# Score matmuls in tiles of 64 by 32 from the third group of heads on, and one pair of vector sums moved behind two copies, in a fused attention and feed-forward kernel

## The chip, the cores and the metric

The kernel runs on one NeuronCore of a Trainium2 chip. The metric is the device time of one execution in microseconds (us). Before the change three runs took 413.71, 417.81 and 420.57 us (median 417.81). The profile is of one further execution, which took 417.34 us.

## The reference, cut to what matters

Attention with normed queries and keys, then a feed-forward layer. Batch 8, 12 heads, 448 positions, head size 64:

```python
q_n, k_n = (rmsnorm(q, g_q), rmsnorm(k, g_k))
scores = scale * np.matmul(q_n, k_n.transpose(0, 1, 3, 2))
scores = scores - np.max(scores, axis=-1, keepdims=True)
attn = np.exp(scores)
attn = attn / (np.sum(attn, axis=-1, keepdims=True) + 1e-09)
x = np.matmul(attn, v)          # to (3584, 768), heads side by side
h = x @ w_in                    # (768, 2048)
g = np.maximum(h, 0.0) + alpha * np.minimum(h, 0.0)
out = g @ w_out                 # (2048, 768)
```

## The kernel before

**Groups.** The unit of attention work is a group `y` of four heads (two heads `par` in each of two halves `g`), 24 groups in all, three to a batch. One call of `score(y, j)` (line 355) makes the scores of the four heads for 64 keys against all 448 queries, into one PSUM tile `sc` of two banks (two such buffers). `soft` (line 373) exponentiates that tile on ScalarE, in one instruction of about 1 us. A group has seven such tiles.

**How a score tile is cut.** In `score`, the stationary operand has 64 rows (the head size) and `m` columns (keys). For groups 0 to 8 (`EARLY` is 9) `m` is 64: four matmuls of form 64*64, one for each head. From group 9 on `m` is 32: eight matmuls of form 64*32. Each moves the same 448 queries, and each is two instructions on TensorE's queue, a weight load and a matmul.

**Sums over the keys.** The denominators (`den`, `den_pre`, lines 419 and 424) and the products with v (`attv`, line 446) are 56 matmuls each, through `over_keys` or `ones_over` (lines 381 and 402), all of them of form 64*32 in every group. `den` puts its sums in the bank pair with tag "acc". `den_pre` is for the third group of a batch, which is handled alone: it puts them in the two single banks with tag "mm" and copies both at once to SBUF on VectorE (line 430), so that those banks come free. Then ScalarE takes logarithm and exponential of the copies (`log_pre`, `invert`), and VectorE multiplies them with the products (line 486, `muls`).

**The feed-forward work.** `up` (matmuls on line 501, form 128*128, tiles `hT`) is followed by a ScalarE and a VectorE instruction; `down` (line 563, `op`) by a VectorE copy and two output DMAs. From batch 2 on, the second product is done in three parts, `quad_a`, `quad_b`, `quad_c` (lines 641 to 692, matmuls on line 628), with seven block products in place of eight. They need sums and differences of blocks of g for each pair of output tiles: `mix_two` (lines 603 to 617) makes `s1` and `s2`, on VectorE in the calls spoken of here, and `mix_rest` (lines 619 to 624) makes two more on GpSimd. `quad_a` uses `s2` in its third product, `quad_b` uses `s1` and one of the GpSimd results. Products and `den_pre` take turns in the same two "mm" banks: a product can't begin before the bank was read out by VectorE.

**The order.** The program is written out by hand for every engine. A planner makes a list of 69 bursts; each has two to four score tiles and at most one step of denominators (`dens`) and one of products with v (`avs`). Between bursts lie feed-forward units (`gaps`), from burst 28 on by a written table (lines 942 to 948). `prep` holds calls that come at a burst's start, ahead of its score tiles, and `jobs` holds VectorE work that is put between other steps. The `mix_two` and `mix_rest` of seven pairs of output tiles are put in `prep` of the bursts 33, 36, 41, 48, 55, 57 and 62 by the loop on line 971. Of these seven bursts only 36 has a `den_pre` (group 11). Its order on VectorE before the change: `mix_two(8)` (two instructions), the two copies of the denominators, two reductions (`jobs`), then what `quad_a(8)` needs.

What calls what around the change, at the start of a burst `n`:

```python
for f, a in prep.get(n, ()):
    f(*a)
...
sums = n in dens and pre(dens[n])
if sums:
    den_pre(dens[n])
    for f, a in jobs.pop(n, ()):
        f(*a)
    ...
    attv(avs[n], 0, False, (log_pre, invert), put, ...)
```

**Loads.** Queries and keys of later groups, v, `w_in` and `w_out` are loaded while the first bursts run: `load_qk` on the queue of SP, `load_v`, `load_w_in` and `load_w_out` on that of GpSimd.

Of the kernel before, what the change touches and what calls it, by code (L numbers as in the profile page):

```python
# [21 lines left out]
def kernel(  # L22
# [12 lines left out]
    nc = tc.nc  # L35
# [15 lines left out]
    EARLY = 3 * G  # L51
# [300 lines left out]
    def pre(ys):  # L352
        return len(ys) == 1 and ys[0] >= PRE and ys[0] % G == G - 1

    def score(y, j):
        qT, kT = qkT[y, "q"], qkT[y, "k"]
        sc = pss.tile([128, 2, 512], FP32, name="sc", tag="sc")
        m = 64 if y < EARLY else 32
        for c in range(64 // m):
            for par in range(2):  # L360
                for g in range(2):
                    nc.tensor.matmul(  # L362
                        out=sc[ds(64 * g + m * c, m), par, :S].rearrange(
                            "p (j c) -> p j c", j=J
                        ),
                        lhsT=kT[ds(64 * par, 64), j, g, ts(c, m)],
                        rhs=qT[ds(64 * par, 64), :, g, :],
                        start=True,
                        stop=True,
                    )  # L370
        scs[y, j] = sc
# [27 lines left out]
    def cols_of(ys):  # L399
        return S // 2 if halved(ys) else S  # L400

    def ones_over(accs, ys):

        if not halved(ys):
            return over_keys(accs, ys, lambda g, y, par, c, j: ones[ds(64 * g, 64)])
        for j in range(J):
            for c in range(2):
                for par in range(2):
                    for g in range(2):
                        p = ds(64 * g, 64)  # L410
                        nc.tensor.matmul(
                            out=accs[g][ds(64 * c + 32 * par, 32), : S // 2],
                            lhsT=ones[p],
                            rhs=expT[ys[0]][p, j, par, ts(c, S // 2)],
                            start=(j == 0),
                            stop=(j == J - 1),
                        )

    def den(ys):
        dn = psa.tile([128, 2, 512], FP32, name="dn", tag="acc")  # L420
        ones_over((dn[:, 0], dn[:, 1]), ys)
        rden[ys] = dn

    def den_pre(ys):
        accs = [psf.tile([128, 512], FP32, name="dnb", tag="mm") for _ in range(2)]
        ones_over(accs, ys)
        r = att.tile([128, 2, S], FP32, name="rden", tag="rden")[:, :, : cols_of(ys)]
        rden[ys] = r
        for g in range(2):
            nc.vector.tensor_copy(out=r[:, g], in_=accs[g][:, : cols_of(ys)])  # L430
# [15 lines left out]
    def attv(ys, half, spare=False, jobs=(), put=None, early=False):  # L446

        b, i = divmod(ys[0], G)
        v2 = vt[b].rearrange("p h j (d e) -> p h j d e", e=2)

        def weights(g, y, par, c, j):
            h = 2 * (y - G * b) + par
            return v2[ds(64 * g, 64), h, j, :, half if len(ys) == 2 else c]

        if half:
            av, accs = None, [psf.tile([128, 512], FP32, name="avb", tag="mm") for _ in range(2)]
        else:
            pool, tag = (pss, "sc") if spare else (psa, "acc")
            av = pool.tile([128, 2, 512], FP32, name="av", tag=tag)
            accs = (av[:, 0], av[:, 1])  # L460
        over_keys(accs, ys, weights)
        for f in jobs:
            f(ys)
        if b not in xT:
            xT[b] = att.tile([128, 2, G, S], FP16, name="xT", tag="xT")
        x, r = xT[b][:, :, i + half, :], rden[ys]
        if half:
            for g in range(2):
                nc.vector.tensor_mul(out=x[:, g], in0=accs[g][:, :S], in1=r[:, g])
        else:  # L470
            parts = [(x, av[:, :, :S], r)]
            if halved(ys):
                parts = [
                    (x[ds(64 * e, 64), :, c], av[ds(64 * e, 64), :, c], r[ds(64 * n, 64)])
                    for n, c in enumerate(ts(n, S // 2) for n in range(2)) for e in range(2)
                ]
            if put is not None:
                soon = 2 if early else 0
                muls(parts[:soon])
                put.append((muls, (parts[soon:],)))  # L480
            else:
                muls(parts)
# [292 lines left out]
    bursts, dens, avs, first_in, last_in = [], {}, {}, {}, {}  # L775
# [5 lines left out]
    m = 0  # L781
    while m < NG * J or steps:
        n = len(bursts)
# [20 lines left out]
        while len(bursts[n]) < limit and m < NG * J:  # L804
            y, j = divmod(m, J)
# [13 lines left out]
    def at(n, f, *a):  # L819
        prep.setdefault(max(int(n), 0), []).append((f, a))  # L820
# [14 lines left out]
    for y in range(G, NG):  # L835

        early = y < G + 2
        if early:
            n = turn_at[y - 1] + 1
        elif y == G + 2:  # L840
            n = den_at[G - 1]
        elif y == 2 * G:
            n = turn_at[y] - 4
        elif y % G == 1:
            n = den_at[y - 4] - 1 - pre((y - 2,))
        elif y % G:
            n = den_at[y - G] - pre((y - G,))
        else:
            n = av_at[y - 4]
# [98 lines left out]
    ).split("|")  # L948
    quads = {"a": quad_a, "b": quad_b, "c": quad_c}

    forced = set()

    def units(line):
        for w in line.split():
# [14 lines left out]
    rest = list(units("b20 c20 u16"))  # L969
    assert not downs and not ups  # L970
    for n, y in ((33, 6), (36, 8), (41, 10), (48, 12), (55, 14), (57, 16), (62, 18)):
        at(n, mix_two, y, nc.vector)
        at(n, mix_rest, y)
    at(65, mix_two, 20, nc.vector, "nat")
# [75 lines left out]
    for n in range(NB):  # L1050
# [6 lines left out]
        for t in first_tiles:  # L1057
            if t == (0, J - 2):
                spin(1)
            elif t == (1, J - 3):  # L1060
                spin(2, False)
            elif t == (1, J - 2):
                spin(1, False)
            elif t == (0, J - 1):
                turn_one(1, "q")
            elif t == (1, 0):
                turn_one(1, "k")
            elif t == (1, J - 1):
                turn(2)
            score(*t)  # L1070
            if n == den_at[G - 1] - 1 and t == tiles[-1]:
                begin(0)
                begin(1)
            elif lead and t == tiles[0]:
                soft(*t)
                den(dens[n])
                attv(avs[n], 0, True, (log, invert))
            elif lead and t == tiles[1]:
                begin(2)
# [11 lines left out]
        sums = n in dens and pre(dens[n])  # L1091
        if sums:
            den_pre(dens[n])
            for f, a in jobs.pop(n, ()):
                f(*a)
            put = [] if not gaps[n] or gaps[n][0][0] in (quad_a, quad_c) else None
            attv(avs[n], 0, False, (log_pre, invert), put, gaps[n] and gaps[n][0][0] is quad_c)
            if not gaps[n]:
                last_jobs, put = [(muls, (p,)) for _, (ps,) in put for p in (ps[:2], ps[2:])], None
            elif put and gaps[n][0][0] is quad_a:  # L1100
                put.insert(0, (lambda: None, ()))
            if put:
                jobs[n] = put + jobs.get(n, [])
        elif n in dens and not lead:
            den(dens[n])
# [4 lines left out]
        for t in () if lead else tiles[len(first_tiles) : 3]:  # L1110
            score(*t)
            soft(*t)
        if n in avs and len(avs[n]) == 2 and avs[n] != (0, 1):
            attv(avs[n], 1)
        for t in () if lead else tiles[max(len(first_tiles), 3) :]:
            score(*t)
            soft(*t)
# [3 lines left out]
        if n in roots:  # L1121
            y = roots[n]
# [112 lines left out]
```

## Time and profile before

| what | us |
|---|---|
| runs before | 413.71, 417.81, 420.57 |
| the profiled execution, its own time | 417.34 |
| its span, first to last instruction | 415.6 |
| outside the span | 1.74 |
| TensorE busy, matmuls | 398.9 (96%), 5055 instructions |
| TensorE weight loads | 208.3 (50%), 5055 instructions |
| VectorE, ScalarE, GpSimd busy | 265.8, 273.4, 255.2 |
| mean granted TensorE clock | 0.994 of full speed |

In the lines of the profile, PE is TensorE, PEld its weight loads, DVE VectorE, ACT ScalarE, POOL GpSimd and SP the engine whose queue issues most DMAs. A line of the timeline gives the start, the time from the first start to the last end, the instructions' engine, line of the kernel, operation, out<-in, form and number, and in brackets how long the engine had been idle before, and what ended that. "issue" stands for a wait that nothing in the profile ended. Ends of matmuls are modelled and overlap the next ones, so the distance from start to start is what a step costs.

### The profile page before, as it was taken

What the parts mean: (1) busy time and instruction counts of PE and PEld (TensorE: products, weight loads), DVE (VectorE), ACT (ScalarE), POOL (GpSimd) and SP (SyncE); (2) the same over time, 40 slices, a digit from 0 to 9 for tenths busy, and PEclk for the clock granted to TensorE, in tenths of its full rate; (3) what the DMA queues carried; (4) which work ended last, traced back from release to release, by engine and by line L of the source; (5) the groups of instructions that cost most, each with busy time, mean ns of one, the idle gap of its engine ahead of it and who ended that gap; (6) DMA issues with size and microseconds to landing.
All of it is one profiled execution on the core that took longest, in us unless ns stands there. A gap on an engine that the chain in (4) does not pass through costs nothing. (4 is left out here: it accounts for less than half of the span.)

```text
span 415.6 us, 11768 instructions
## 1 busy us (share of the span) xinstructions
PE 398.9 (96%) x5055; PEld 208.3 (50%) x5055; DVE 265.8 (64%) x421; ACT 273.4 (66%) x390; POOL 255.2 (61%) x180
## 2 busy tenths in 40 slices
PE   6889899999999999989999999999999999999996
PEld 3344345544455445544455445444555445655564
DVE  3876675575556485795788585958577755465322
ACT  4798697778956785666786897884667884135110
POOL 5589695779596974887094857476633507400870
PEclk9899999999999999999999999999999999999999
DMA  8999999976827596829957596279412800320133
GB/s 182 238 234 229 162 210 168 231 193 88 178 36 177 136 125 112 182 64 175 141 81 175 130 211 139 67 167 193 95 41 48 141 4 21 77 58 0 38 95 96
DMA packets 68019, 53.39 MB, mean 128 GB/s; under 512 B 35568, under 2 KB 67456, under 8 KB 67968
## 3 DMA queue, kind: packets, MB, share of 16 engines
q1 hardware_dynamic: 53520, 39.54, 45.5%
q0 software_dynamic: 13472, 11.81, 20.0%
q10 hardware_dynamic: 976, 1.31, 1.3%
q8 instruction: 39, 0.64, 0.7%
q14 instruction: 12, 0.10, 0.1%
HBM read 45.62 MB, written 11.01 MB: 136 GB/s over the span
## 5 line engine op out<-in xcount | busy, mean ns | idle before, releaser
L376 ACT ACTIVATE expT<-sc,expb 128x896 f16<-128x896 f32 x168 | 162.2, 1003 | 45.9 <-PE sc L362 45.7
L501 PE MATMUL hT<-xT,w_in_sb 128*128 128x448 f16 x546 | 113.7, 353 | 2.1 <-issue 1.7
L501 PEld LDWEIGHTS <-w_in_sb 128*128 128x128 f16 x768 | 72.7, 98 | 76.6 <-issue 12.3
L545 DVE TENSOR_TENSOR gT<-hT,gT 128x448 f16<-128x448 f32 x91 | 56.6, 623 | 40.3 <-ACT gT L541 39.2
L210 POOL TENSOR_TENSOR qs<-nat,rr 128x896 f16<-128x896 f32 x36 | 60.5, 1702 | 34.7 <-issue 21.8
L182 POOL TENSOR_TENSOR sq<-nat 128x896 f32<-128x896 f32 x32 | 53.5, 1683 | 41.8 <-DMA nat<-in_q_dram 29.6
L541 ACT ACTIVATE gT<-hT,cols 128x448 f16<-128x448 f32 x90 | 56.9, 633 | 30.0 <-PE hT L501 29.7
L362 PE MATMUL sc<-qT,kT 64*32 64x448 f16 (+1 forms) x1092 | 53.7, 358 | 4.3 <-ACT expT L376 2.0
L628 PEld LDWEIGHTS <-gT 128*128 128x128 f16 x352 | 33.5, 98 | 26.8 <-issue 5.7
L501 PE MATMUL hTa<-xT,w_in_sb 128*128 128x448 f16 x210 | 45.4, 353 | 0.0
L190 DVE TENSOR_REDUCE ss<-sq 128x14 f32<-128x896 f32 (+1 forms) x37 | 38.5, 1052 | 0.9 <-POOL sq L182 0.8
L486 DVE TENSOR_TENSOR xT<-av,rden 64x448 f16<-64x448 f32 (+1 forms) x37 | 27.2, 734 | 14.2 <-PE av L387 8.9
L545 DVE TENSOR_TENSOR gT<-hTa,gT 128x448 f16<-128x448 f32 x35 | 21.8, 623 | 19.5 <-ACT gT L541 19.2
L541 ACT ACTIVATE gT<-hTa,cols 128x448 f16<-128x448 f32 x35 | 22.2, 635 | 18.2 <-PE hTa L501 18.1
L362 PEld LDWEIGHTS <-kT 64*32 64x32 f16 (+1 forms) x1092 | 16.0, 93 | 36.0 <-issue 29.9
L563 PE MATMUL op<-w_out_sb,gT 128*128 128x384 f16 x160 | 27.4, 326 | 0.0
L387 PEld LDWEIGHTS <-vt 64*32 64x32 f16 x1344 | 19.9, 92 | 12.4 <-issue 2.8
L616 POOL TENSOR_TENSOR gs<-gT 128x1024 f16<-128x1024 f16 x3 | 6.4, 2125 | 30.4 <-DVE gT L545 28.1
L563 PEld LDWEIGHTS <-gT 128*128 128x128 f16 x192 | 18.0, 98 | 13.4 <-issue 2.3
L387 PE MATMUL av<-expT,vt 64*32 64x448 f16 x896 | 24.3, 350 | 0.3 <-DVE osb L676 0.3
L624 POOL TENSOR_TENSOR gT<-gT 128x1024 f16<-128x1024 f16 x11 | 23.4, 2128 | 0.0
L628 PE MATMUL qx<-w_out_sb,gT 128*128 128x384 f16 x120 | 20.8, 326 | 1.2 <-DVE rden L430 1.2
(149 smaller groups left out, 494.0 us busy)
## 6 DMA issues: line engine op xcount, KB each, us to landing
out_dram<-osb SPq DMA_DIRECT2D x107, 96.0 KB, 3.0
nat<-in_q_dram SPq DMA_DIRECT2D x40, 224.0 KB, 4.2
nat<-in_k_dram SPq DMA_DIRECT2D x40, 224.0 KB, 5.1
vt<-in_v_dram POOLq DMA_DIRECT2D x16, 336.0 KB, 8.0
w_in_sb<-in_moe_w_in_dram POOLq DMA_DIRECT2D x12, 256.0 KB, 7.8
w_out_sb<-in_moe_w_out_dram POOLq DMA_DIRECT2D x4, 768.0 KB, 9.7
arena<-in_q_dram SPq DMA_DIRECT2D x6, 224.0 KB, 7.4
arena<-in_k_dram SPq DMA_DIRECT2D x6, 224.0 KB, 6.8
```

The source lines that it names most:

```text
L182: nc.gpsimd.tensor_mul(out=sqf[:, c], in0=src[:, c], in1=src[:, c])
L190: nc.vector.tensor_reduce(out=o[:, c], in_=sqs[y, nm][:, c], axis=AXIS_X, op=ALU.add)
L210: eng.tensor_mul(out=t.rearrange("p j h d -> p h j d"), in0=nat[y, nm], in1=rr_t[y][:, "qk".index(nm)].unsqueeze(3).broadcast_to((128, 2, ...
L362: nc.tensor.matmul(out=sc[ds(64 * g + m * c, m), par, :S].rearrange("p (j c) -> p j c", j=J), lhsT=kT[ds(64 * par, 64), j, g, ts(c, m)], r ...
L376: nc.scalar.activation(out=expT[y][:, j], in_=scs[y, j][:, :, :S], func=AF.Exp, scale=QK_SCALE, bias=expb[:, 0:1],)
L387: nc.tensor.matmul(out=accs[g][ds(32 * n, 32), :S], lhsT=weights(g, y, par, c, j), rhs=expT[y][ds(64 * g, 64), j, par, :], start=(j == 0), ...
L486: nc.vector.tensor_mul(out=x, in0=av, in1=r)
L501: nc.tensor.matmul(out=hT[:, :S], lhsT=w_in_sb[:, g * G + i, ts(ft, 128)], rhs=xT[b][:, g, i, :], start=(i == 0 and g == 0), stop=(i == G ...
L541: nc.scalar.activation(out=g, in_=hT[:, :S], func=AF.Copy, scale=alpha_sb[:, ft : ft + 1])
L545: nc.vector.tensor_max(out=g, in0=hT[:, :S], in1=g)
L563: nc.tensor.matmul(out=op[:, :OH], lhsT=gT[:, ft, ts(tile % J, 128)], rhs=w_out_sb[:, ft, ts(oh, OH)], start=(ft == 0), stop=(ft == NF - 1),)
L628: nc.tensor.matmul(out=bank[:, c], lhsT=g[:, ft], rhs=v[:, ft, c], start=(first and ft == 0), stop=(ft == HF - 1), skip_group_check=True,)
```

## The change

Two edits. `score` uses 64*64 tiles for groups 0 and 1 alone; groups 2 to 8 (49 score tiles) are cut as the later groups were. And in a burst that has a `den_pre`, the pair `mix_two`, `mix_rest` is no longer called at the burst's start but right behind `den_pre`, that is behind the two copies on VectorE and ahead of the burst's `jobs`. This is the case in burst 36 alone.

```diff
     def score(y, j):
         qT, kT = qkT[y, "q"], qkT[y, "k"]
         sc = pss.tile([128, 2, 512], FP32, name="sc", tag="sc")
-        m = 64 if y < EARLY else 32
+        m = 64 if y < 2 else 32
         for c in range(64 // m):
...
-    forced = set()
+    forced, behind = set(), {}
...
     for n, y in ((33, 6), (36, 8), (41, 10), (48, 12), (55, 14), (57, 16), (62, 18)):
+        if n in dens and pre(dens[n]):
+            behind[n] = [(mix_two, (y, nc.vector)), (mix_rest, (y,))]
+            continue
         at(n, mix_two, y, nc.vector)
         at(n, mix_rest, y)
...
         sums = n in dens and pre(dens[n])
         if sums:
             den_pre(dens[n])
+            for f, a in behind.pop(n, ()):
+                f(*a)
             for f, a in jobs.pop(n, ()):
                 f(*a)
```

## The prediction

> **What bounds the kernel now.** I read the page's busy times, then TensorE's timeline from end to end, then VectorE's and GpSimd's around burst 36, then counts of instructions by window and the DMA queues.
>
> ```profile
> PE 398.9 (96%) x5055; PEld 208.3 (50%) x5055; DVE 265.8 (64%) x421; ACT 273.4 (66%) x390; POOL 255.2 (61%) x180
> DMA  8999999976827596829957596279412800320133
> q8 instruction: 39, 0.64, 0.7%
> ```
>
> TensorE is busy 96% and no other engine over 66%: what shortens TensorE's stream shortens the kernel, and each of its waits lengthens it. DMA is full for the first 83 us (eight slices of 10.4 us). The queue that brings instructions had 39 packets (16 KB each).
>
> TensorE's timeline, once with 64*64 scores around denominators and once with 64*32 scores:
>
> ```profile
> 68.67 0.57 PE L362 MATMUL sc<-qT,kT 64*64 64x448 f16 x8
> 69.17 1.52 PE L387 MATMUL dn<-expT,ones 64*32 64x448 f16 x56
> 70.62 0.38 PE L362 MATMUL sc<-qT,kT 64*64 64x448 f16 x4
> 70.93 2.77 PE L563 MATMUL op<-w_out_sb,gT 128*128 128x384 f16 x16
> ```
>
> ```profile
> 157.21 0.57 PE L362 MATMUL sc<-qT,kT 64*32 64x448 f16 x16
> 157.60 1.51 PE L387 MATMUL dn<-expT,ones 64*32 64x448 f16 x56
> 158.92 0.37 PE L362 MATMUL sc<-qT,kT 64*32 64x448 f16 x8
> 159.23 2.77 PE L563 MATMUL op<-w_out_sb,gT 128*128 128x384 f16 x16
> ```
>
> Start to start the same work takes 70.93 - 68.67 = 2.26 us above and 159.23 - 157.21 = 2.02 below: each border between the two forms costs 0.12 us. Between 128*128 work both forms cost the same: two tiles take 0.50 us start to start either way.
>
> Burst 36, TensorE and VectorE:
>
> ```profile
> 177.72 0.57 PE L362 MATMUL sc<-qT,kT 64*32 64x448 f16 x16
> 179.50 2.76 PE L628 MATMUL qx<-w_out_sb,gT 128*128 128x384 f16 x16 [1.21 <-DVE rden L430]
> 185.93 1.46 PE L628 MATMUL qz<-w_out_sb,gT 128*128 128x384 f16 x8 [0.32 <-DVE osb L657]
> ```
>
> ```profile
> 176.26 2.09 DVE L616 TENSOR_TENSOR arena<-gT 128x1024 f16<-128x1024 f16 x1
> 178.45 0.69 DVE L617 TENSOR_TENSOR arena<-arena,gT 128x1024 f16<-128x1024 f16 x1
> 179.06 0.68 DVE L430 COPY rden<-dnb 128x224 f32<-128x224 f32 x2
> 179.66 2.07 DVE L190 TENSOR_REDUCE ss<-sq 128x14 f32<-128x896 f32 x2
> ```
>
> The product waits for the copies, which stand behind `mix_two`. The longest wait after the start-up is another:
>
> ```profile
> 36.28 0.63 PE L362 MATMUL sc<-qT,kT 64*64 64x448 f16 x4
> 43.33 0.92 PE L501 MATMUL hT<-xT,w_in_sb 128*128 128x448 f16 x4 [1.72 <-issue]
> ```
>
> ```profile
> 36.40:43.20 6.80, 5.21 (x128) 2.56 (x128) 1.59 (x2) 3.77 (x4) 6.67 (x8) 1.00 1.14 218
> ```
>
> At 43.33 TensorE waits though its data is there (xT, line 486, ended at 41.45). At 36.28 a score tile takes 0.63 where others take 0.38: its second weight load comes 0.25 us late. Between the two stoppings lie 128 matmuls and 128 weight loads, 256 instructions exactly; counted from the start they are numbers 705 and 961 of TensorE's queue. An instruction packet began 33.76 and took 1.17 us (TensorE went on 1.59 after its end); the next began 40.87 and took 0.94 (went on 1.52 after). So TensorE's instructions come in blocks of 256; a block is asked for when the one before it is begun, and under full DMA comes about 6.8 us later. Numbers 705 + 256k are the borders; the other packets fit this to the end.
>
> **The change part by part.**
>
> *Borders removed.* From 68 us on, where TensorE otherwise doesn't wait: two around the denominators at 69.17; four around the two sums 74.14 and 75.90 (4.03 us, the same block at 165.83 takes 3.53); two each at 81.09, 85.41 and 111.22; three at 118.79 and 120.55. Fifteen by 0.124 = 1.86 us. Two of these places also hold waits of 0.15 and 0.18 for VectorE, which would grow by what is saved; I take 1.7 (ends 1.5 and 1.86). The borders before 43 us I cost at nothing: the waits for ScalarE's exponentials and for instructions cover them.
>
> *Instructions added.* 49 tiles by 4 matmuls and 4 weight loads are 392. In time they cost nothing between 128*128 work (0.50 against 0.50), and no DMA of the data is added. But every block of 256 now reaches less far in the program.
>
> Block at 705: five tiles of group 2 come before it (40 instructions), so it now begins at what was number 665, a transpose at 33.43. It is asked for at the same place as before, within 0.3 us (29.5 for 29.7), behind the same loads, so TensorE goes on at about 36.2. Then: three transposes, two score tiles, eight `hT` matmuls, group 3's tile; the denominators need two exponentials of 1.0 us behind those score tiles, and start at 38.8 (36.84 before); they and two thirds of the sums with v (1.32 + 0.9) lead to number 961, now what was 897, at 41.0. The next block was asked for at 36.2 and, by the earlier 6.8 us, is there at 43.1. What then still lies before the `hT` of 43.33: 19 matmuls of sums (0.45), a score tile (0.31), eight `hTb` matmuls (1.51). It starts at 45.4: +2.1 us. Ends: 0, if the block comes 2.8 us sooner; 3.0, if it comes as much later as packets differ (0.9).
>
> Block at 1729: 26 tiles come before it, so it begins at what was 1521, at 73.67, just before the sums of 74.14, where instructions go fastest; it ends at what was 1761, at 77.35, after 3.7 us. A block is asked for some 23 instructions ahead of its border (an estimate, from packets that began before TensorE reached theirs). The packets of the two borders nearest (70.62 and 76.70) began at 74.48 and 80.72, 4.35 and 4.24 after that point. Asked for at 73.1, with 4.2 + 0.97 + 1.55 it is there at 79.8: TensorE waits +2.4 us. Ends 0 and 3.0.
>
> The other borders keep a slack of 0.5 us or more by the packets nearest in time, but for one: block 165.84 to 169.07. There DMA is idle from 163 to 167 us, and a packet under idle DMA (120.90, asked for at 120.55) came 0.35 later; with 1.2 and 1.55 that is 168.9, just in time. I take 0; ends 0 and 0.9.
>
> *Burst 36.* `mix_two` and, on GpSimd, `mix_rest` move past the two copies and nothing else; no DMA moves, GpSimd's order stays (its squares until 177.80 come first). The sums of the denominators end at 176.4, so the copies (0.38 each, as in the five other bursts) run at 176.6 to 177.3. `mix_two`'s first took 2.09 here, 0.69 in other bursts; it ended 0.55 after GpSimd's square ended (177.80). It still ends near 178.35, the second at 179.1. So `mix_rest` is no later. The first product starts at 178.2, not 179.50: 1.28 sooner. But VectorE is solid: reductions 179.1 to 181.1, then the copy of the first product at 181.05 (181.64 before), which frees the bank of the third (181.65 for 182.24), and so on to the wait at 185.93. What is late next is VectorE's own row, and the gain left is the copies' 0.6 us. Ends: 0 and 1.6 (both waits gone).
>
> *Sum.* 417.34 (span 415.6 and 1.74 around it) + 2.1 + 2.4 - 1.7 - 0.6 = 419.5 us. The profiled execution is 0.5 below the median of the runs shown, 417.81.
>
> **The rivals.**
>
> *Instructions come in time.* Blocks are asked for sooner in the new order and both waits stay away or merge into the one at 43.33: 417.34 - 1.86 - 0.6 = 414.9. For it: only two of 39 borders stop TensorE now. Against: both are stopped with no slack left (0.25 and 1.87 us), and the new blocks are 2.8 and 3 us shorter in time. It decides once a block comes within 3.7 us of its asking. [...]
>
> *One of the two stays away.* 419.5 - 2.1 or - 2.4: about 417.2. The first is better founded (it stands on a stop that exists), the second on two packets near by.
>
> *Slower: a clock stage on top.* From 7.90 to 11.31 us TensorE was busy 1.07 of 3.41 us, and from 11.31 to 14.73 the granted clock was 0.50. If the wait at 77.35 leaves a stretch of 3.41 us as empty, the next 3.41 run at half: +1.7, 421.2. Against: the wait is 2.4 us, so at least 1.0 us of the stretch is busy and it must fall so; the least busy stretch afterwards, 2.12 (42.03 to 45.45), kept 1.00. The first wait can trip it too, but the second block's arrival covers that.
>
> **How the numbers follow.** Both waits 0.50 (419.5; its own range 417.5 to 421.5), one of them 0.22 (417.2), none 0.17 (414.9), with a clock stage 0.11 (421.2). With the ends of the terms these reach from 414 to 423; 414.5 to 422.5 leaves out less than 2 in 10. A measurement of this kernel can tell about 2% from no change, 8.4 us: none of the cases goes so far, so faster 0.01, same 0.97, slower 0.02.
>
> **What would show it.** Scores of group 2 on as 64*32, PE x5251; the denominators of 69.17 with 1.32 for 1.45 from start to start. An "issue" wait of 2 to 3 us on transposes near 33.5, one in sums (`av`) near 41, one on a score tile or `opa` near 79. In burst 36 the two copies right behind the denominators and ahead of L616, and `qx` without its 1.21. Wrong: if there is no wait by "issue" between 75 and 85 us, the second term goes; if `hT` still starts near 43.3, the first.

## The result, and the profile after

The changed kernel takes 420.16 us (median of 20 runs, 416.63 to 421.05), the kernel before, run beside it, 416.78 us (20 runs, 413.06 to 420.57). The ratio is 1.0087, interval 1.0065 to 1.0110: slower by 0.9%, 3.4 us between the medians, and inside the 2%. The forecast of 419.5 us lay 0.7 below the median. Here and below, medians are over all runs, while ratios leave disturbed runs out and are not quotients of these medians, so that the two can differ by up to 0.3%.

The profiled execution of the changed kernel took 416.63 us (span 414.9). It is the shortest of the 20, so what the change did can't be read from its end. Stages are compared below over several profiles, from landmarks that leave the start-up out (the first denominators start at 26.06 us here and at 27.54 in the profile before).

The page after, first line of part 1, and the instruction queue:

```profile
PE 396.5 (96%) x5251; PEld 209.1 (50%) x5251; DVE 264.4 (64%) x421; ACT 272.8 (66%) x390; POOL 255.4 (62%) x180
q8 instruction: 41, 0.67, 0.7%
```

5251 matmuls are 196 more, 49 tiles by four, and two more packets of instructions come. TensorE's busy time falls by 2.4 us and the others' hardly move, so what is lost must be waits.

TensorE's timeline, changed kernel, around the first two borders:

```profile
31.51 0.79 PE L335 MATMUL tps<-ident,arena 128*128 128x128 f16 x11
34.40 0.34 PE L335 MATMUL tps<-ident,arena 128*128 128x128 f16 x3 [2.10 <-issue]
...
38.32 1.12 PE L387 MATMUL av<-expT,vt 64*32 64x448 f16 x37
40.59 0.74 PE L387 MATMUL av<-expT,vt 64*32 64x448 f16 x19 [1.15 <-issue]
...
42.98 0.92 PE L501 MATMUL hT<-xT,w_in_sb 128*128 128x448 f16 x4
```

Counted from the start, the first instruction after each "issue" wait is number 705 and number 961 of TensorE's queue. They fall on the transposes and in the sums with v that the prediction named, and the `hT` that stood behind the old wait of 1.72 now starts with none. Two waits of 2.10 and 1.15 us are there in place of 0.25 and 1.72. This `hT` starts at 42.98, close to its 43.33 before; but counted from the first denominators it is 16.92 us, 15.79 before.

The same view, at the denominators and at the third border:

```profile
68.32 0.57 PE L362 MATMUL sc<-qT,kT 64*32 64x448 f16 x16
68.71 1.51 PE L387 MATMUL dn<-expT,ones 64*32 64x448 f16 x56
70.03 0.37 PE L362 MATMUL sc<-qT,kT 64*32 64x448 f16 x8
70.34 2.77 PE L563 MATMUL op<-w_out_sb,gT 128*128 128x384 f16 x16
...
76.29 0.35 PE L362 MATMUL sc<-qT,kT 64*32 64x448 f16 x1
77.17 0.38 PE L362 MATMUL sc<-qT,kT 64*32 64x448 f16 x7 [0.53 <-issue]
```

Scores, denominators and scores now take 70.34 - 68.32 = 2.02 us (2.26 before): two borders between forms less, 0.12 each. The stop in the score tile is number 1985 (705 + 5 x 256). There the block ends that the prediction calls the one at 1729, and the expectations below name the stop by that number.

Burst 36, TensorE, first the denominators in the kernel before, then the changed kernel:

```profile
175.66 0.85 PE L411 MATMUL dnb<-expT,ones 64*32 64x224 f16 x56
```

```profile
175.85 0.85 PE L411 MATMUL dnb<-expT,ones 64*32 64x224 f16 x56
...
178.41 2.77 PE L628 MATMUL qx<-w_out_sb,gT 128*128 128x384 f16 x16
181.86 1.46 PE L628 MATMUL qx<-arena 128*128 128x384 f16 x8 [0.68 <-DVE osb L647]
...
185.53 1.46 PE L628 MATMUL qz<-w_out_sb,gT 128*128 128x384 f16 x8 [0.31 <-DVE osb L657]
```

and VectorE:

```profile
176.81 0.69 DVE L430 COPY rden<-dnb 128x224 f32<-128x224 f32 x2 [0.29 <-PE dnb L411]
177.42 1.14 DVE L616 TENSOR_TENSOR arena<-gT 128x1024 f16<-128x1024 f16 x1
...
179.27 2.07 DVE L190 TENSOR_REDUCE ss<-sq 128x14 f32<-128x896 f32 x2
```

The copies run first and the first product has no wait (1.21 before). Half of it comes back at the third product, 0.68 behind VectorE's copy of the first. From the denominators to the second `qz` it is 185.53 - 175.85 = 9.68 us, 185.93 - 175.66 = 10.27 before: 0.6 gained, as forecast.

One wait is new that the prediction doesn't name. TensorE around 137 us in the kernel before, then TensorE, VectorE and GpSimd in the changed kernel:

```profile
128.49 1.19 PE L411 MATMUL dnb<-expT,ones 64*32 64x224 f16 x56
137.12 1.31 PE L501 MATMUL hT<-xT,w_in_sb 128*128 128x448 f16 x6
```

```profile
135.68 0.57 PE L362 MATMUL sc<-qT,kT 64*32 64x448 f16 x16
137.16 1.30 PE L501 MATMUL hT<-xT,w_in_sb 128*128 128x448 f16 x6 [0.91 <-DVE osb L574]
```

```profile
130.80 1.08 DVE L190 TENSOR_REDUCE ss<-sq 128x14 f32<-128x896 f32 x1 [1.31 <-POOL sq L182]
133.00 1.09 DVE L190 TENSOR_REDUCE ss<-sq 128x14 f32<-128x896 f32 x1 [1.11 <-POOL sq L182]
134.00 2.52 DVE L486 TENSOR_TENSOR xT<-av,rden 64x448 f16<-64x448 f32 x4
136.55 1.02 DVE L574 COPY osb<-op 128x384 f32<-128x384 f32 x2
```

```profile
129.09 1.68 POOL L182 TENSOR_TENSOR sq<-nat 128x896 f32<-128x896 f32 x1 [2.63 <-DMA nat<-in_q_dram]
131.28 1.68 POOL L182 TENSOR_TENSOR sq<-nat 128x896 f32<-128x896 f32 x1 [0.52 <-DMA nat<-in_k_dram]
```

Burst 28's denominators start at 127.55 (128.49 before); nine microseconds later TensorE stands at the same point as before, 137.16 (137.12). Read back: the bank of `hT` comes free by a copy, which stands behind the multiplications, these behind two reductions, these behind GpSimd's squares, and these wait for loads. In this pair of profiles TensorE gave its lead back to work that doesn't depend on it. The wait doesn't belong to the small tiles alone: in the experiments below TensorE waits 0.79 us there with the second edit alone, and not at all with the first edit alone.

### The profile page after: what moved, and what is told of

Its sections match the earlier page's. It is cut to its first block, busy times and chain, and to the rows that moved or that the text cites. A ratio compares the mean times of both kernels' runs of the same rounds, so it can differ in the third digit from the quotient of the medians.

```text
span 414.9 us, 12160 instructions
## 1 busy us (share of the span) xinstructions
PE 396.5 (96%) x5251; PEld 209.1 (50%) x5251; DVE 264.4 (64%) x421; ACT 272.8 (66%) x390; POOL 255.4 (62%) x180
## 3 DMA queue, kind: packets, MB, share of 16 engines
q10 hardware_dynamic: 976, 1.31, 1.3%
## 5 line engine op out<-in xcount | busy, mean ns | idle before, releaser
L210 POOL TENSOR_TENSOR qs<-nat,rr 128x896 f16<-128x896 f32 x36 | 60.5, 1700 | 37.5 <-issue 21.7
L545 DVE TENSOR_TENSOR gT<-hT,gT 128x448 f16<-128x448 f32 x91 | 56.6, 623 | 38.2 <-ACT gT L541 37.3
L545 DVE TENSOR_TENSOR gT<-hTa,gT 128x448 f16<-128x448 f32 x35 | 21.8, 624 | 19.5 <-ACT gT L541 19.2
L616 POOL TENSOR_TENSOR gs<-gT 128x1024 f16<-128x1024 f16 x3 | 6.4, 2119 | 30.4 <-DVE gT L545 28.1
```

The costliest lines, as they stand in the source:

```text
L210: eng.tensor_mul(out=t.rearrange("p j h d -> p h j d"), in0=nat[y, nm], in1=rr_t[y][:, "qk".index(nm)].unsqueeze(3).broadcast_to((128, 2, ...
L545: nc.vector.tensor_max(out=g, in0=hT[:, :S], in1=g)
```

## The experiments

The theory after this: the loss is in the two blocks ahead of 43 us, through group 2's 56 added instructions; the border gain is real and is given back to the loads, squares and reductions. The rivals: small tiles cost by their number; any added instruction costs; the wait at 137 is VectorE's order alone. Every ratio is to the kernel before on the same chip.

### The two edits apart, and the whole again

Second edit alone (the kernel before with the lines for `behind`):

> Only the second edit: the sums of g behind the copies in burst 36, score tiles as before. Theory (the edits are separate; VectorE is the next bound in burst 36): 0.6 us faster than before, ratio 0.9985; qx without its wait of 1.21 us, the first blocks of instructions as before (a wait at the hT of 43.3, none on the transposes near 34). Rival (both waits of burst 36 go): 1.6 us faster. Rival (the late sums cost something on GpSimd): slower, up to 1 us.

Measured 415.67 against 415.69, ratio 1.0003 (0.9975 to 1.0031). Inconclusive: 0.6 us would be 0.9986, inside the interval. In its profile the wait for VectorE ahead of the first product is gone, but after two of its matmuls another stands there:

```profile
179.66 2.45 PE L628 MATMUL qx<-w_out_sb,gT 128*128 128x384 f16 x14 [0.64 <-issue]
```

This is number 4545 of the queue, 705 + 15 x 256, so again a border of a block. With 0.72 more at the third product the stage takes 10.46 us, no less than before. The kernel before with only the reductions of burst 28 moved (below) has an "issue" wait of 0.94 us at the same instruction.

First edit alone:

```diff
-        m = 64 if y < EARLY else 32
+        m = 64 if y < 2 else 32
```

> Only the first edit: 64 by 32 tiles from group 2 on, the sums of g as before. Theory (the loss is the tiles', through instruction blocks): slower than before by what the whole change loses and the second edit gains, 3.4 + 0.6 = 4.0 us, ratio 1.0095; waits by issue at queue numbers 705, 961 and 1729. Rival (the second edit is what loses): about 1.7 us faster than before by the borders alone.

Measured 419.69, ratio 1.0111 (1.0064 to 1.0157). All of the loss is the first edit's. Its profile has "issue" waits of 2.26, 1.42 and 0.46 us at the same three instructions.

The changed kernel again, on another chip:

> The changed kernel once more, for a second profile of it: the one at hand is of its fastest run (416.63 us where the median is 420.16). Theory (instruction blocks): the waits at queue numbers 705, 961 and 1729 are there again, together longer than the 3.8 us of the first profile if the run is nearer to the median; ratio 1.0087. Rival (another, rarer wait makes the median): a wait that the first profile doesn't have.

Measured 420.24 against 416.48, ratio 1.0079 (1.0051 to 1.0106); waits of 2.81, 0.41 and 1.38 us.

### Which tiles cost

Group 2 alone in small tiles, and no second edit:

```diff
-        m = 64 if y < EARLY else 32
+        m = 64 if y < EARLY and y != 2 else 32
```

> 64 by 32 tiles for group 2 alone, ahead of 43 us, and for groups 9 on as before; the sums of g as before. No border after 68 us is removed; 28 matmuls more. Theory (56 more instructions ahead of 36 us move the block borders): the wait on a transpose near 34 us and the one in the sums av near 41 are there as in the changed kernel, 1 to 2.9 us slower than before. Rival (it is the many tiles of groups 3 to 8, or the tile form itself, that costs): no difference, since seven score tiles can't cost 1 us.

Measured 419.09 against 415.69, ratio 1.0092 (1.0056 to 1.0127): seven tiles of 49 cost as much as all, as far as these intervals tell. TensorE in this kernel:

```profile
34.63 0.34 PE L335 MATMUL tps<-ident,arena 128*128 128x128 f16 x3 [2.30 <-issue]
...
35.79 2.94 PE L501 MATMUL hT<-xT,w_in_sb 128*128 128x448 f16 x8
```

and its windows (us, PE busy and count, then the other engines, granted clock, DMA share, GB/s):

```profile
34.60:35.80 1.20, 1.17 (x20) 0.34 (x21) 0.79 (x2) 0.26 (x1) 1.20 (x2) 0.65 1.17 295
35.80:38.60 2.80, 2.80 (x16) 1.03 (x8) 1.88 (x2) 1.65 (x2) 2.80 (x4) 0.54 1.11 243
38.60:41.70 3.10, 3.10 (x117) 1.68 (x116) 0.00 (x0) 2.11 (x3) 3.10 (x4) 1.00 1.19 203
```

After the wait the granted clock is 0.65 and 0.54 in the two windows up to 38.6 us: the eight `hT` take 2.94 here and 1.69 in the changed kernel's profile.

All groups but 2 (both edits, from group 3 on); then from 4 and from 6 on, with these numbers in place of the 3:

```diff
-        m = 64 if y < 2 else 32
+        m = 64 if y < 3 else 32
```

> Both edits with small tiles from group 3 on: 42 of the 49 tiles, only group 2 left as it was. Theory, that the loss is group 2's 56 instructions, which move two borders of 256 into places where TensorE is quicker than its instructions: issue waits as in the kernel before (one near 43 us), ratio 0.998 to 1.003, the upper end if the border that now lies near 77 us still costs its 0.5 us. Rival, that the loss grows with the number of small tiles: six sevenths of it, 1.007.

Measured 418.07 against 415.57, ratio 1.0039 (1.0004 to 1.0075). The ratio lies between the two, about half the loss, and its interval holds the ends of both (1.003 and 1.007). The waits are not those of the kernel before. It is again a block ahead of 43 us; group 3's first two tiles (16 instructions) shift number 961 from `hT` into `hTb`:

```profile
38.39 0.36 PE L501 MATMUL hTb<-xT,w_in_sb 128*128 128x448 f16 x1
41.78 2.80 PE L501 MATMUL hTb<-xT,w_in_sb 128*128 128x448 f16 x7 [3.04 <-issue]
44.37 1.70 PE L501 MATMUL hT<-xT,w_in_sb 128*128 128x448 f16 x4
```

A wait of 3.04 us, and half clock behind it (granted clock 0.50 from 41.8 to 46.0 us; four `hT` in 1.70, 0.92 at full clock). No "issue" wait stands near 77 us in this profile.

> Both edits, 64 by 32 tiles from group 4 on (35 tiles, 280 instructions more, behind 49 us). Theory: nothing early; all fifteen borders gone (1.86 us); the block that begins near 72 us lies 16 score tiles earlier than before and can cost 0 to 2 us near 77 us; between 1.5 us faster and 1 us slower than before. Rival (it is the number of 64 by 32 tiles): 35/49 of the loss, 2.4 us slower.

Measured 416.80 against 416.48, ratio 0.9998 (0.9973 to 1.0023): 35 small tiles cost nothing and bring nothing that can be measured; the rival's 2.4 us (1.0058) is excluded. Its one early wait:

```profile
41.79 0.92 PE L501 MATMUL hT<-xT,w_in_sb 128*128 128x448 f16 x4 [0.49 <-issue]
```

> Both edits, but 64 by 32 tiles from group 6 on instead of group 2 (21 tiles, 168 instructions more, all behind 70 us). Theory (the loss comes from the blocks at 705 and 961): those two as in the kernel before, no wait on a transpose near 34; ten of the fifteen borders gone (1.24 us), of which up to 1 us can be lost again at the hT of 137 us, which e1, e3 and e4 show waiting for VectorE whenever TensorE comes early; 0 to 1.6 us faster than before, ratio 0.996 to 1.0. Rival (64 by 32 scores cost by themselves): 21/49 of the loss, 1.5 us slower.

Measured 418.11 against 416.48 as medians, ratio 1.0009 (0.9981 to 1.0037): no difference that can be told. The interval holds both the theory's 1.0 and the rival's 1.5 us (1.0036).

### Instructions without the change of form

The work before, and 40 more instructions in the warm-up ahead of the first score tile (four large idle matmuls replaced by 24 small ones):

```diff
-    spin(17, False)
+    spin(13, False)
+    filler = psf.tile([128, 512], FP32, name="filler", tag="mm")
+    for n in range(24):
+        nc.tensor.matmul(
+            out=filler[ds(32 * (n % 4), 32), :S], lhsT=ones[ds(0, 64)], rhs=idle[ds(0, 64)],
+            start=True, stop=True,
+        )
```

> The kernel before, every score tile and sum as it was; in the warm-up ahead of 9 us four of 17 idle matmuls are replaced with 24 short ones of form 64*32 (the same time, 40 more instructions in TensorE's queue). Theory (blocks of 256 instructions): the block of number 705 begins 40 instructions earlier in the program, at the transposes near 33.4, the next in the sums av near 41; 1 to 3 us slower than before, though nothing but idle matmuls changed. Rival (the loss has to do with the score tiles, their form or their order): no difference.

Measured 418.36, ratio 1.0070 (1.0040 to 1.0101). No score tile changed, and most of the loss is there. The stop is on the same transposes:

```profile
34.39 0.34 PE L335 MATMUL tps<-ident,arena 128*128 128x128 f16 x3 [1.02 <-issue]
```

The price isn't seen in this profile. It is of 416.70 us, the shortest of the 12 runs, and has no other early "issue" wait; from the first denominators to the first `op` it takes 37.58 us, less than the 38.43 of the kernel before.

216 instructions in place of 40 (no `spin(17)`, 125 small matmuls of 288 columns):

> The kernel before, all its work as it was; in the warm-up ahead of 9 us the 17 idle matmuls are replaced with 125 short ones of 64*32 (about the same time, 216 more instructions, five times as many more as in e4). Theory (only the place of the 256-borders counts): 216 puts the borders where the old ones were less 40 the other way, into dn near 37 us and beyond 43.3: the waits of 0.25 and 1.72 us by issue are gone, hT near 41.5; not slower than before, 0 to 1.9 us faster, of which the wait for VectorE at 137 us can take all. Rival (more instructions ahead cost more, as e4 could also be read): slower by five times e4's 2.7 us, or at least as much as e4.

Measured 418.60 against 416.48, ratio 1.0037 (1.0002 to 1.0071). In time a miss. It isn't five times the 40's loss, so the number of instructions alone doesn't set the price; that added instructions cost something wherever the borders lie isn't excluded. Its profile has no "issue" wait between 20 and 45 us, as forecast. Later TensorE waits 0.87 us at 92.84 and 2.81 at the `hT` of 139.23, both for VectorE. But this execution, 421.75 us, was its longest, so that these waits needn't be what the other executions lose; why this kernel is slower stays open.

### The wait at 137 us

The reductions of burst 28 are put behind its multiplications, in three kernels:

```diff
-            for f, a in jobs.pop(n, ()):
-                f(*a)
+            if n != 28:
+                for f, a in jobs.pop(n, ()):
+                    f(*a)
...
             attv(avs[n], 0, False, (log_pre, invert), put, gaps[n] and gaps[n][0][0] is quad_c)
+            for f, a in jobs.pop(n, ()) if n == 28 else ():
+                f(*a)
```

In the changed kernel:

> The changed kernel, with the two reductions of burst 28 on VectorE (line 190) put behind the four multiplications of the same burst (line 486) instead of ahead of them. Theory, that what TensorE won from 68 us on was given back at the hT of 137 us because the multiplications and the copies that free its banks stand behind reductions, which wait for GpSimd's squares and these for loads: the wait of 0.91 us at 137.16 goes, and the kernel is 0.3 to 0.9 us faster than the changed one, ratio to the kernel before about 1.006 (the changed kernel had 1.0087 and 1.0079). Rival, that the loads themselves are the floor: the reductions' results are late next, TensorE waits as long within the following 10 us, ratio still about 1.008.

Measured 419.34 against 415.57, ratio 1.0093 (1.0062 to 1.0124). The theory's 1.006 lies just outside the interval, the rival's 1.008 inside. `hT` has no wait at 137.82, and TensorE waits 0.80 us at 154.13 instead, for VectorE's L545, which is later than the 10 us that the rival gave. Since the first edit alone had no wait at this `hT` either, with its reductions in their old place, one profile can't show that the move took it away.

With small tiles from group 4 on:

> Both edits with small tiles from group 4 on (which had ratio 0.9998 with a wait of 0.27 us at that hT in its profile), and the same two reductions behind the multiplications. Theory: the borders that were removed from 68 us on (1.5 us) are kept if nothing waits at 137: ratio 0.996 to 0.999. Rival, that the loads are the floor: 1.000, with a new wait between 137 and 150 us.

Measured 416.82 against 415.57, ratio 1.0019 (0.9988 to 1.0049). The rival's 1.000 fits, and of the theory's range only the upper end, 0.999, is left. TensorE, then VectorE, then GpSimd of this kernel:

```profile
149.44 0.57 PE L362 MATMUL sc<-qT,kT 64*32 64x448 f16 x16
152.12 1.92 PE L501 MATMUL hT<-xT,w_in_sb 128*128 128x448 f16 x6 [2.10 <-DVE gT L545]
153.84 2.40 PE L501 MATMUL hTa<-xT,w_in_sb 128*128 128x448 f16 x6
```

```profile
149.92 1.09 DVE L190 TENSOR_REDUCE ss<-sq 128x14 f32<-128x896 f32 x1 [2.48 <-POOL sq L182]
150.92 0.61 DVE L545 TENSOR_TENSOR gT<-hTa,gT 128x448 f16<-128x448 f32 x1
```

```profile
146.59 1.66 POOL L596 TENSOR_TENSOR w_out_sb<-w_out_sb 128x768 f16<-128x768 f16 x1
148.20 3.32 POOL L182 TENSOR_TENSOR sq<-nat 128x896 f32<-128x896 f32 x2
```

The next reduction stands ahead of L545 and waits 2.48 us for the next squares; these end a stretch in which GpSimd works without a gap from 129.00. TensorE still waits for VectorE, 15 us further on.

In the kernel before:

> The kernel before, with only the two reductions of burst 28 behind the multiplications. In its profile the hT of 137.12 had no wait. Theory: nothing to win, ratio 1.000 (0.998 to 1.002). Rival, that this order of VectorE costs the kernel before as well, in executions whose first part is quicker: 0.997 to 0.999.

Measured 416.01 against 415.57, ratio 1.0008 (0.9974 to 1.0043): nothing to win that can be measured, as the theory had it; the rival's 0.998 and 0.999 lie in the interval too.

What the loads wait for is seen on SP's queue, changed kernel, with its longest waits between 100 and 130 us (total, times, longest):

```profile
121.64 1.24 SPq L309 DMA_TRANSPOSE qT<-qs  x1
123.29 1.22 SPq L309 DMA_TRANSPOSE kT<-qs  x1
124.56 1.25 SPq L127 DMA_DIRECT2D nat<-in_q_dram  x2
```

```profile
SPq L309 <- POOL qs L210: 15.9, 3, 8.7
```

The loads are queued behind transposes that wait for GpSimd's scaling (L210), up to 8.7 us; GpSimd's next squares wait for the loads. That would be a ring of GpSimd and SP with a pace of its own. It is argued from what the profile infers to have ended each wait; no run made the ring itself faster.

No kernel here beats the one before by a measurable amount.

## Why the prediction was right, point by point

**Blocks of 256: right.** The waits stand at numbers 705, 961 and 1985 in the changed kernel and again in its repeat. Group 2's 56 instructions alone, and 40 idle ones, bring most of the loss in the medians with no or few score tiles changed.

**First term, +2.1 us: right in size over several profiles.** From the first denominators to the first `op`, the four profiles with all 49 tiles (the changed kernel, its repeat, the first edit alone, the reductions moved) take 39.57, 40.82, 39.73 and 40.68 us, mean 40.20. The four with unchanged work up to there (the kernel before, the second edit alone, before with the reductions moved, small tiles from group 6 on) take 38.43, 38.15, 37.24 and 38.34, mean 38.04. That is +2.16; the first pair of profiles alone has +1.14. Group 2 alone takes 40.19, and the 40 idle instructions, as said, 37.58. Number 705 went on at 34.40, with a start-up 1.48 earlier than before's; the forecast was 36.2. Number 961 was running 6.2 us after number 705 (34.40 to 40.59), against 6.8 assumed. That number 705's start asks for it is the prediction's estimate, from when packets begin; no trace shows an asking.

**"The first wait can trip it too, but the second block's arrival covers that": half right.** Half clock followed the first wait in the repeat, in group 2 alone and with the reductions moved (the eight `hT` behind it took 2.44, 2.94 and 2.72 us, against 1.69 at full clock). In group 2 alone `av` then had no wait, so it was covered. With all tiles, number 705 to number 961 takes 6.74 us in both profiles at half clock, and 6.19 and 6.46 in the two at full clock: most of it is covered, and the 0.3 to 0.6 more may be what isn't. The rival with the clock had it at 77 us; it came at 36.

**Second term, +2.4 us: mis-sized.** The wait is there in all four profiles: 0.53, 0.46, 1.38 and 0.82, mean 0.8. The step that failed is the time of arrival, taken from the two neighbouring packets: in the changed kernel's first profile the packet began 2.3 us after the point at which the prediction's estimate has it asked for (72.47 to 74.75; 3.1 in the repeat), not 4.2, and ran 4.7 after, not 6.7.

**Borders between forms, -1.7 us: made by 128 us, and not found in the times.** From the first `op` to burst 28's denominators, unchanged work takes 62.52, 62.51 and 62.90 (mean 62.64), all 49 tiles 61.92, 61.85, 62.78 and 62.21 (mean 62.19). Without the 0.8 of waits that is -1.25. The kernels from groups 3 and 4 on, with no wait in this stretch, take 61.05 and 61.04: -1.6; the one from group 4 on with the reductions moved takes 61.93, with 0.59 of "issue" wait in it. From group 4 on the gain is there and the first term is not, and the time is that of before: 1.5 us would be 0.9964, outside both intervals. The prediction let the gain go through to the end; it didn't ask what sets the pace of loads, squares and reductions.

Where the gain goes isn't shown. In the first pair the wait at 137 took 0.9 us. Over several profiles the small tiles lose nothing there: from burst 28's denominators to burst 36's, the three with unchanged tiles take 47.17, 49.26 and 48.24 us, the four with all 49 tiles 48.30, 47.18, 47.98 and 48.03.

**Second edit, -0.6 us: right for the profile it was worked out from, about nothing on the whole.** From burst 36's denominators to the second `qz`, the old order takes 10.27, 10.17, 10.14, 10.11, 9.01 and 9.00 us in six profiles, the new one 9.18, 9.18, 9.20, 9.22, 9.68, 9.68, 10.32 and 10.46 in eight. The old order isn't slow whenever it runs, nor the new one always quick. VectorE in the kernel with the 40 idle instructions:

```profile
177.18 0.68 DVE L616 TENSOR_TENSOR arena<-gT 128x1024 f16<-128x1024 f16 x1
177.97 0.69 DVE L617 TENSOR_TENSOR arena<-arena,gT 128x1024 f16<-128x1024 f16 x1
178.57 0.68 DVE L430 COPY rden<-dnb 128x224 f32<-128x224 f32 x2
```

TensorE reached the burst 0.9 us later there, the addition L616 began after one square of GpSimd had ended (176.81) and took 0.68 in place of 2.09, and the first product had no wait at all. The prediction took the collision of one execution for a property of the kernel.

**The sum.** +2.2, +0.8, -1.25 and about 0 make +1.7 by 128 us. From burst 28's denominators to the last ones of a third group, near 357 us, the profiles with all tiles take no longer (229.82, 230.28, 229.02 and 230.69 us, against 229.58, 231.56 and 230.20). The profiled executions as a whole agree with this: the four with all tiles took 418.3 us in the mean, the three unchanged ones 416.9, so 1.4 more. The medians say 3.4. So more than half of what the medians lose isn't seen in these profiles; with all tiles, three of the four are of their kernels' shortest or second shortest run. That 419.5 came so near to 420.16 was in part luck: it is 2.2 us above the execution it was added to, where 3.4 was measured; that execution lay 0.6 above the median of the kernel before; the second term was 1.6 too high; and a gain of 1.7 was counted that the times don't show.

**The rivals.** "Instructions come in time" is excluded: every profile with all tiles waits by "issue" at 705 and 1985, and all but that with the reductions moved at 961 too. "One of the two stays away" comes nearest as to the wait behind the block at 1729, a third of its price.

**Open.** What the median loses beyond the profiles; what sets the pace of the ring; and how far the loss splits into waits and half clock, since executions of one kernel differ by 4 us. After 150 us other waits of 0.7 to 1.4 us come and go (among them `avb` at 215 to 216 in the first edit alone and in both kernels with small tiles and the reductions moved); they weren't taken apart.

## What to carry to other kernels

Where TensorE waits by "issue", count instructions from the start and look what lies at each such wait. In the changed kernel the waits stood multiples of 256 apart (numbers 705, 961, 1985); added instructions changed what lay there, and their number alone didn't set the price: 40 ahead of the first score tile had ratio 1.0070, 216 there 1.0037, and 280 behind 49 us (small tiles from group 4 on) 0.9998. A gain in the busiest engine needn't reach the end: with small tiles from group 4 on 1.6 us were gained by 128 us, and the ratio is 0.9998. So follow the first wait that could take a gain back before adding it to a sum. And a collision of two engines seen in one execution (L616 took 2.09 us in one profile, 0.68 in another) should be asked for in a second one before its removal is priced. The same holds for a loss: in the first pair of profiles here the changed kernel's execution was the shorter by 0.7 us, where the medians of 20 runs lost 3.4.

## What the runs showed of the hardware

**Half clock after a wait of 2.1 us.** The windows of the kernel with small tiles from group 4 on and the reductions moved (us, PE busy and count, granted clock, DMA share, GB/s):

```profile
149.80:152.10 2.30, 0.22 (x16) 1.00 1.28 142
152.10:153.80 1.70, 1.68 (x6) 0.66 1.38 140
153.80:156.10 2.30, 2.30 (x8) 0.51 1.17 250
156.10:158.40 2.30, 2.30 (x13) 1.00 1.08 220
```

2.10 us of wait here and 2.30, 2.66, 2.81 and 3.04 in four others (group 2 alone, the changed kernel with the reductions moved, the changed kernel again, small tiles from group 3 on) brought half clock; 2.10 in the changed kernel's profile, 2.26 with the first edit alone, and 2.81 and 2.25 with the 216 instructions (ending at 139.23 and 288.97) did not. So the length of the wait doesn't decide it. These stretches at half clock last 3.41 us in the clock's record (6.83, twice that, after the wait of 3.04). Count steps of 3.41 us from the start of such a stretch: the step just before it held 1.31, 1.12, 1.27, 1.10 and 1.25 us of busy TensorE in the five, and around the four waits without half clock the emptiest step held 1.74, 2.17, 1.65 and 2.10. It is no threshold, since at 20.55 us, with the first edit alone, half clock followed a step with 2.23. What decides it isn't shown.

**A VectorE addition under GpSimd's squares.** L616 took 0.68 us where no square ran, 2.09 in the profile before and 1.14 after; in both it ended 0.55 us after the square (178.35 and 177.80; 178.56 and 178.01). What holds the addition so long isn't shown.
